# Loads, sums and row 0 of the first batch: another order in the prologue of a Fourier mixing and SwiGLU kernel

## The chip, the cores and the metric

The kernel runs on one core of a Trainium2 chip. Times are device microseconds (us) of that core. A "run" is one execution; a profile is one run with the hardware profiler on, and its span is some 2 us shorter than its time. Names: TensorE (PE; PEld its weight loads), VectorE (DVE), ScalarE (ACT), GpSimd (POOL), SyncE (SP, which here only issues DMA).

For a program on one core no die stands beside it to compare, so besides the time I always look at the **mean granted clock** of TensorE: 1.000 if it had full clock all the time, 0.997 with one stretch of half clock of 3.4 us in some 618 (half of 3.4/618 is 0.0028), 0.994 with two.

## The reference

```python
X = np.fft.fft(x, axis=1)            # x: 8 x 3008 x 256
X = np.fft.fft(X, axis=2)
x = X.real.astype(np.float32).reshape(8 * 3008, 256)
g = x @ w_gate                       # 256 x 1536
silu = g * (1.0 / (1.0 + np.exp(-g)))
return (silu * (x @ w_val)) @ w_out  # 24064 x 256
```

## The kernel before

The transform over the sequence is folded by symmetry (middle blocks XA and XC), then done with tables of cosines and sines; the transform over the 256 columns is multiplied into the weights (Wp, Wq, Wm). Then units of 512 tokens by 128 hidden columns go through TensorE, ScalarE (Silu) and VectorE, products hp and hm are multiplied with Wo, and ScalarE copies the output from PSUM into one of three buffers (ev), from which SyncE stores it. GpSimd folds the later batches and makes some of the products hm.

The prologue, where the change is (SyncE's queue is `q`; cuts are marked). `place` sends a block through TensorE in passes that reverse its order; a chunk is a slice of the weights that one load brings; `halves` makes bf16 copies of the sums:

```python
    for hi, what, eng in ((1, 2, nc.scalar), (0, 2, q), (0, 0, q), (1, 0, q), (0, 1, q), (1, 1, q)):
        eng.dma_start(**xc0(hi, what))                    # block XC of batch 0
    q.dma_start(out=XC0[NCR:64 + NCR + 1:64, 0:2, 1],     # row 0 of batch 0
                in_=rows_at(0, 0, [[2 * R * D, 2], [R * D, 2], [1, D]]))
    for hi in range(2):
        for k in range(2):                                # zero fill for the next batch's XC
            q.dma_start(out=X3c[64 * hi + NCR:64 * hi + 64, 8 * D * k:8 * D * (k + 1)],
                        in_=xf[NCR + 1:NCR + 2, :].unsqueeze(1).to_broadcast([1, 64 - NCR, 8 * D]))
    # ... (SyncE's next instructions are the next batch's XC loads)
    psA = place(XA, putA, 4, ((psG, "g"), (psV, "v")))    # TensorE reverses XA through PSUM
    warm(20)
    sums(SA, 0, XA, psA)                                  # VectorE
    # ...
    load_w(0, (1,))                                       # GpSimd's queue: weight chunks
    # ...
    weigh(0, NCE)                                         # VectorE
    psC = place(XC0, putC, 2, ((psO, "o"),))
    # ...
    load_w(1)
    sums(SC, 0, XC0, psC)
    halves(SBc, SC, 0)                                    # ScalarE
```

Two places further on matter for what follows. In the first units VectorE also makes a table of odd angles, with two operations from SBUF to SBUF:

```python
    def weigh(lo, hi):
        vts(Tab[:, 1, 1, :, lo:hi], Tab[:, 1, 1, :, lo:hi], scalar1=wC, scalar2=None, op0=Alu.mult)
    def odd_table(c, half):                               # four times
        nc.vector.tensor_copy(Tab[r, c, :, :, NCE:NCE + GH], src[:, :, ::-1] if half else src)
```

And SyncE issues in program order: one XA load of batch 1, the load br (a row of tile Qt, so after the "Qt puts", VectorE's writes to Qt), 15 more XA loads, bc, XC loads for batches 2 and 3, and among them the output stores. GpSimd's folds of XA and XC wait for those loads.

## Time and profile before

Three runs: 620.09, 620.14 and 622.67 us, median 620.14. The head of the page:

```profile
span 618.3 us, 12468 instructions
## 1 busy us (share of the span) xinstructions
PE 601.1 (97%) x4008; PEld 393.7 (64%) x4069; DVE 582.6 (94%) x1062; ACT 528.3 (85%) x1005; POOL 469.9 (76%) x430
```

TensorE is busy for 97% of the span, and from 113 to 600 us for 483.8 of 487 us; in the timeline of that stretch its idle times add up to 0.4 us (some matmul records are missing). So whatever happens, happens in the first fifth of the kernel:

| stretch | what sets the pace |
|---|---|
| to 25.57 us | the prologue; block XC waits for row 0, then goes at half clock |
| 25.57 to about 53 | VectorE, busy 23.94 of 24.43 us up to 50 |
| about 53 to 113 | TensorE nearly full, with some holes |
| from 113 | TensorE full |

One thing about the column "busy", which the rest of this document turns on: an instruction that is held up after it has started counts as busy (the same one took 0.42 us alone and 1.93 us held, below).

### The profile page before, as it was taken

What the parts mean: (1) busy time and instruction counts of PE and PEld (TensorE: products, weight loads), DVE (VectorE), ACT (ScalarE), POOL (GpSimd) and SP (SyncE); (2) the same over time, 40 slices, a digit from 0 to 9 for tenths busy, and PEclk for the clock granted to TensorE, in tenths of its full rate; (3) what the DMA queues carried; (4) which work ended last, traced back from release to release, by engine and by line L of the source; (5) the groups of instructions that cost most, each with busy time, mean ns of one, the idle gap of its engine ahead of it and who ended that gap; (6) DMA issues with size and microseconds to landing.
All of it is one profiled execution on the core that took longest, in us unless ns stands there. A gap on an engine that the chain in (4) does not pass through costs nothing.

```text
span 618.3 us, 12468 instructions
## 1 busy us (share of the span) xinstructions
PE 601.1 (97%) x4008; PEld 393.7 (64%) x4069; DVE 582.6 (94%) x1062; ACT 528.3 (85%) x1005; POOL 469.9 (76%) x430
## 2 busy tenths in 40 slices
PE   6989999999999999999999999999999999999997
PEld 4546665666666666666666666666666666666676
DVE  9699889899999999999999999999999999999992
ACT  6686666889889889998898899998998988999993
POOL 8798679899787989986988769876887344437552
PEclk9999999999999999999999999999999999999999
DMA  9843646355414323454145112135111121111112
GB/s 229 135 68 76 165 111 187 109 142 131 135 56 128 93 62 112 139 120 129 54 105 128 51 55 78 52 86 148 54 51 52 45 61 44 52 45 53 59 52 78
DMA packets 50588, 57.68 MB, mean 93 GB/s; under 512 B 7234, under 2 KB 37578, under 8 KB 50506
## 3 DMA queue, kind: packets, MB, share of 16 engines
q1 hardware_dynamic: 46915, 53.75, 31.5%
q0 software_dynamic: 3184, 2.36, 2.8%
q10 hardware_dynamic: 423, 0.77, 0.4%
q8 instruction: 32, 0.52, 0.4%
q14 instruction: 34, 0.28, 0.2%
HBM read 29.39 MB, written 24.65 MB: 87 GB/s over the span
## 4 chain that ended last, share of the span: by engine, by line
PE 84%; DVE 7%; DMA 3%; ACT 3%; issue 2%; POOL 1%; SPq 0%; DVEq 0%; ACTq 0%
PE o L1148 35%; PE g L908 23%; PE v L908 19%; DVE es L1031 2%; DMA out_dram<-ev 2%; PE g L1291 2%; PE o L1291 2%; DVE sv L1092 2%; DMA XA<-in_x_dram 1%; ACT sv L1078 1%; DVE hp L1102 1%; PE o L411 1%; POOL EOA L478 1%; PE v L1148 0%; PE o L578 0%
## 5 line engine op out<-in xcount | busy, mean ns | idle before, releaser
L1099 POOL TENSOR_TENSOR hm<-sv 128x1024 bf16<-128x1024 f32 (+2 forms) x133 | 247.5, 1861 | 119.8 <-ACT sv L1078 73.1
L1092 DVE SCALAR_TENSOR_TENSOR sv<-es,v 128x512 f32<-128x512 f32 (+2 forms) x266 | 178.5, 672 | 3.4 <-PE v L908 2.5
L1102 DVE TENSOR_TENSOR hp<-sp,v 128x512 bf16<-128x512 f32 (+2 forms) x260 | 174.6, 672 | 3.5 <-ACT sp L1075 2.2
L1148 PE MATMUL o<-Wo,hm 128*128 128x256 bf16 (+1 forms) x1128 | 166.6, 273 | 0.6
L1148 PE MATMUL o<-Wo,hp 128*128 128x256 bf16 (+1 forms) x1104 | 165.4, 273 | 0.4
L1148 PEld LDWEIGHTS <-hm 128*128 128x128 bf16 (+2 forms) x1140 | 112.0, 98 | 60.4 <-issue 0.2
L1148 PEld LDWEIGHTS <-hp 128*128 128x128 bf16 (+2 forms) x1140 | 112.1, 98 | 58.4 <-issue 1.3
L1006 ACT ACTIVATE sp<-g 128x512 f32<-128x512 f32 (+2 forms) x198 | 119.3, 603 | 30.3 <-PE g L908 19.7
L1078 ACT ACTIVATE sv<-g 128x512 f32<-128x512 f32 (+2 forms) x198 | 129.3, 655 | 5.0 <-PE g L908 3.9
L908 PE MATMUL v<-Pt,Wp 128*128 128x512 bf16 (+2 forms) x284 | 106.4, 375 | 3.8 <-DVE hm L966 1.4
L908 PE MATMUL g<-Pt,Wp 128*128 128x512 bf16 (+2 forms) x284 | 106.4, 375 | 0.7 <-DVE Qt L1308 0.3
L1031 DVE SCALAR_TENSOR_TENSOR es<-bc,w,v 128x512 f32<-128x512 bf16 (+2 forms) x140 | 102.3, 732 | 1.4 <-PE v L908 1.1
L908 PE MATMUL g<-Qt,Wq 128*128 128x512 bf16 (+2 forms) x242 | 90.3, 374 | 0.3
L980 ACT ACTIVATE v<-bc,w 128x512 f32<-128x512 bf16 (+2 forms) x126 | 87.2, 692 | 0.5 <-DVE hp L1102 0.3
L908 PE MATMUL g<-Qt,Wm 128*128 128x512 bf16 (+2 forms) x217 | 81.3, 375 | 0.6 <-ACT sp L1006 0.2
L1029 ACT COPY es<-v 128x512 f32<-128x512 f32 (+2 forms) x126 | 74.0, 587 | 2.7 <-PE v L908 2.3
L908 PEld LDWEIGHTS <-Wp 128*128 128x128 bf16 x576 | 56.2, 98 | 30.9 <-issue 5.3
L1154 ACT COPY ev<-o 128x512 f32<-128x512 f32 x89 | 53.6, 602 | 9.1 <-PE o L1148 4.7
L908 PE MATMUL v<-Qt,Wq 128*128 128x512 bf16 (+2 forms) x159 | 59.5, 375 | 0.2
L908 PEld LDWEIGHTS <-Wq 128*128 128x128 bf16 x450 | 44.0, 98 | 23.6 <-issue 2.4
L908 PE MATMUL v<-Qt,Wm 128*128 128x512 bf16 (+2 forms) x148 | 55.4, 374 | 0.6 <-DVE hp L946 0.6
L1010 DVE SCALAR_TENSOR_TENSOR sg<-bc,w,g 128x512 f32<-128x512 bf16 (+2 forms) x68 | 49.6, 729 | 0.3 <-POOL hp L1111 0.3
(187 smaller groups left out, 702.5 us busy)
## 6 DMA issues: line engine op xcount, KB each, us to landing
out_dram<-ev SPq DMA_DIRECT2D x96, 128.0 KB
XA<-in_x_dram SPq DMA_DIRECT2D x30, 256.0 KB
XA<-in_x_dram SPq DMA_DIRECT2D x112, 64.0 KB
XC<-in_x_dram SPq DMA_DIRECT2D x32, 120.0 KB
XC<-in_x_dram SPq DMA_DIRECT2D x105, 32.0 KB
bc<-br SPq DMA_DIRECT2D x21, 128.0 KB
St<-Fc SPq DMA_DIRECT2D x14, 128.5 KB
out_dram<-ev SPq DMA_DIRECT2D x12, 120.0 KB
```

Of the source, the lines that this page charges most:

```text
L908: nc.tensor.matmul(ps[:, :n], Wt[:, gv, fs], src[:, :n], start=start, stop=stop, skip_group_check=True)
L980: nc.scalar.activation(T_[kv][:, :w], bc[t][:, :w], AF.Copy, scale=w0[:, 1, f:f + 1])
L1006: nc.scalar.activation(T_[ksp][:, :w], T_[kg][:, :w], AF.Silu)
L1010: nc.vector.scalar_tensor_tensor(T_[keg][:, :w], bc[t][:, :w], w0[:, 0, f:f + 1], T_[kg][:, :w], op0=Alu.mult, op1=Alu.add)
L1029: nc.scalar.copy(T_[kes][:, :w], T_[kv][:, :w])
L1031: nc.vector.scalar_tensor_tensor(T_[kes][:, :w], bc[t][:, :w], w0[:, 1, f:f + 1], T_[kv][:, :w], op0=Alu.mult, op1=Alu.add)
L1078: nc.scalar.activation(sv()[:, f % 2, w - 1::-1, 1], T_[kgm if by_dve else kg][:, :w], AF.Silu)
L1092: nc.vector.scalar_tensor_tensor(sv()[:, f % 2, w - 1::-1, 0], T_[kes][:, :w], 2.0, T_[kv][:, :w], op0=Alu.mult, op1=Alu.subtract)
L1099: nc.gpsimd.tensor_tensor(hts_(t)[1][:, f - 1:f + 1, :w], sv()[:, :, :w, 1], sv()[:, :, :w, 0], op=Alu.mult)
L1102: nc.vector.tensor_tensor(hts_(t)[0][:, f, :wp], T_[ksp][:, :wp], T_[kv][:, :wp], op=Alu.mult)
L1148: nc.tensor.matmul(st["ps"][:n, j, :], hts[t][minus][:, f, c:c + n], Wo[:, f, :], start=(f == 0), stop=(f == nF - 1))
L1154: nc.scalar.copy(ev[:, 0:len(pair), :], st["ps"][:, 0:len(pair), :])
```

## The change

The intent: block XC of batch 0 comes earlier, because its loads are short pieces on two queues and row 0 goes by GpSimd's queue; VectorE folds it straight from PSUM; small work goes to ScalarE; the zero fill and so the next batch's loads come later. The core of the diff:

```diff
-    q.dma_start(out=XC0[NCR:64 + NCR + 1:64, 0:2, 1],
-                in_=rows_at(0, 0, [[2 * R * D, 2], [R * D, 2], [1, D]]))
-    (zero fill: four DMAs out of XC0)
+    rise_c(0, q)
+    fall_c(1, 0, nc.scalar)
+    fall_c(1, 1, nc.scalar)
+    rise_c(1, q)
+    fall_c(0, 0, q)
+    fall_c(0, 1, q)
 ...
+    nc.gpsimd.dma_start(out=XC0[NCR:64 + NCR + 1:64, 2:4, 0],
+                        in_=rows_at(0, 0, [[2 * R * D, 2], [R * D, 2], [1, D]]))
 ...
+    weigh_ce()                 (ScalarE; was weigh(0, NCE) on VectorE)
+    warm(8)
+    psC = place(XC0, putC, 2, ((psG, "g"), (psV, "v")))
 ...
-    sums(SC, 0, XC0, psC)
-    halves(SBc, SC, 0)
+    direct(0)                  (VectorE, PSUM to the bf16 halves)
+    direct(1)
+    nc.gpsimd.memset(zeros, 0.0)
+    for hi in range(2):
+        q.dma_start(out=X3c[64 * hi + NCR:64 * hi + 64, :].rearrange("p (c d) -> p c d", d=D),
+                    in_=zeros[64 * hi + NCR:64 * hi + 64].unsqueeze(1).to_broadcast([64 - NCR, 16, D]))
 ... (sums of SC, half_folded(1), load_w(1), load_w(2), heads and turns stand later;
      both Wm halves of the first weight chunk go from GpSimd to ScalarE)
```

From the first feed-forward unit on every engine's instruction order is the same in both kernels.

More of the change, by code (lines that the diff above doesn't have):

```diff
@@ L240, with fall_a, rise_c, fall_c @@
     q.dma_start(out=XA3[:, 0:4, :], in_=up_block(0, 1, P))
-    nc.scalar.activation(w0[:, 0, 0:1], zero, AF.Silu)
-    nc.scalar.dma_start(out=XA3[:, 7, :], in_=down_set(0, 3, JA, LA, NA))
-    for k in range(2):
-        nc.scalar.copy(xf[:, 4 * D * k:4 * D * (k + 1)], zero.to_broadcast([P, 4 * D]))
-    for a, eng in ((2, q), (1, nc.scalar), (0, q)):
-        eng.dma_start(out=XA3[:, 4 + a, :], in_=down_set(0, a, JA, LA, NA))
+    def fall_a(a, eng):
+        eng.dma_start(out=XA3[:, 4 + a, :], in_=down_set(0, a, JA, LA, NA))
+    def rise_c(hi, eng):
+        eng.dma_start(out=XC3[64 * hi:64 * hi + 64, 0:2, :],
+                      in_=rows_at(0, 2 * (P + 1) - 1 + 2 * hi * R, [[2 * D, 64], [R * D, 2], [1, 2 * D]]))
+    def fall_c(hi, a, eng):
+        eng.dma_start(out=XC3[64 * hi:64 * hi + NCR, 2 + a, :], in_=down_set(0, 3 - 2 * hi - a, JC, LC, NC_))
+    nc.scalar.activation(w0[:, 0, 0:1], zero, AF.Silu)
+    fall_a(3, nc.scalar)
+    nc.scalar.copy(xf[:, 4 * D:8 * D], zero.to_broadcast([P, 4 * D]))
+    fall_a(2, q)
+    fall_a(1, nc.scalar)
+    fall_a(0, q)
+    rise_c(0, q)
[4 more added lines that the diff above has]
+    fall_c(0, 1, q)
     iota = dict(channel_multiplier=0, allow_small_or_imprecise_dtypes=True)
@@ L257 @@
     nc.gpsimd.iota(pcol2, pattern=[[0, 1]], base=P, channel_multiplier=1, allow_small_or_imprecise_dtypes=True)
-    def xc0(hi, what):
-        if what == 2:
-            return dict(out=XC3[64 * hi:64 * hi + NCR, 0:2, :],
-                        in_=rows_at(0, 2 * (P + 1) - 1 + 2 * hi * R, [[2 * D, NCR], [R * D, 2], [1, 2 * D]]))
-        return dict(out=XC3[64 * hi:64 * hi + NCR, 2 + what, :], in_=down_set(0, 3 - 2 * hi - what, JC, LC, NC_))
-    for hi, what, eng in ((1, 2, nc.scalar), (0, 2, q), (0, 0, q), (1, 0, q), (0, 1, q), (1, 1, q)):
-        eng.dma_start(**xc0(hi, what))
-    q.dma_start(out=XC0[NCR:64 + NCR + 1:64, 0:2, 1],
-                in_=rows_at(0, 0, [[2 * R * D, 2], [R * D, 2], [1, D]]))
-    X3c = XC.rearrange("p a q d -> p (a q d)")
-    for hi in range(2):
-        for k in range(2):
-            q.dma_start(out=X3c[64 * hi + NCR:64 * hi + 64, 8 * D * k:8 * D * (k + 1)],
-                        in_=xf[NCR + 1:NCR + 2, :].unsqueeze(1).to_broadcast([1, 64 - NCR, 8 * D]))
     for i, c_ in enumerate((pcol, pcol2)):
@@ L282, in more_iotas @@
             nc.gpsimd.iota(putC[:, pm - NCR:pm], pattern=[[-LC, NC_], [1, LC]], base=pm - LC, **iota)
-            nc.gpsimd.memset(putC[:, pm:pm + 1], float(pm))
         pts(putC, putC, scalar1=pcol, scalar2=1.0, op0=Alu.is_equal, op1=Alu.mult)
@@ L288 @@
         ps = psO.tile([P, T], F32, name="o")
-        for j in range(10):
+        for j in range(13):
             nc.tensor.matmul(ps[:, 0:P], sel, sel, start=True, stop=True)
@@ L325 @@
     vts(sgn, half, scalar1=1.0 / 32, scalar2=1.0, op0=Alu.mult, op1=Alu.add)
+    sgo = const.tile([P, 1], F32, name="sgo")
+    vts(sgo, pc, scalar1=float(NCR), scalar2=-2.0, op0=Alu.is_equal, op1=Alu.mult)
+    vts(sgo, sgo, scalar1=1.0, scalar2=sgn, op0=Alu.add, op1=Alu.mult)
     vts(wC, pc, scalar1=float(LC - 1), scalar2=-0.5, op0=Alu.is_equal, op1=Alu.mult)
@@ L354, in opposite, with weigh_ce @@
         nc.scalar.activation(Tab[:, ch, :, :, NCE:NOO - 1], Tab[:, ch, :, :, GH + 1:NCE], AF.Copy, scale=-1.0)
+    def weigh_ce():
+        nc.scalar.activation(Tab[:, 1, 1, :, 0:NCE], Tab[:, 1, 1, :, 0:NCE], AF.Copy, scale=wC)
     def load_w(fc, only=(0, 1)):
@@ L414, in place, with sums @@
         return pss
-    def sums(S, k, X, pss):
+    def sums(S, k, X, pss, only=None):
         n = len(pss)
-        for a in range(n):
+        for a in only or range(n):
             down = X[:, 7 - a] if n == 4 else X[:, 2 + a]
@@ L447, in half_w @@
             nc.scalar.copy(dst[:, :, fs], ps)
-            pts(Wm[:, :, fs], dst[:, :, fs], scalar1=m2, scalar2=1.0, op0=Alu.mult, op1=Alu.mult)
         else:
@@ L506, in first_rows, with direct @@
         nc.scalar.copy(w0.rearrange("p g f -> p (g f)"), ps[:, 0:2 * nF])
+    def direct(k):
+        for a in range(2):
+            down = XC0[:, 2 + a, ::-1, :]
+            for hf, r_ in ((0, slice(P, 0, -1)), (1, slice(P, D))):
+                x_, y_ = psC[a][:, :, r_], down[:, :, r_]
+                if k and hf:
+                    x_, y_ = y_, x_
+                vtt(SBc[:, k, hf, a], x_, y_, op=(Alu.add, Alu.subtract)[k])
     psA = place(XA, putA, 4, ((psG, "g"), (psV, "v")))
     warm(20)
-    sums(SA, 0, XA, psA)
+    sums(SA, 0, XA, psA, (0, 1, 2))
+    sums(SA, 1, XA, psA, (0,))
+    sums(SA, 0, XA, psA, (3,))
     opposite(0)
-    for a in (0, 2):
-        fold_d(0, a)
+    fold_d(0, 0)
+    weigh_ce()
+    fold_d(0, 2)
+    opposite(1)
     load_w(0, (1,))
     d_tables()
-    sums(SA, 1, XA, psA)
+    sums(SA, 1, XA, psA, (1, 2, 3))
     start_acc(0)
     half_folded(0, 0)
-    weigh(0, NCE)
-    opposite(1)
-    psC = place(XC0, putC, 2, ((psO, "o"),))
+    warm(8)
+    psC = place(XC0, putC, 2, ((psG, "g"), (psV, "v")))
     half_folded(0, 2)
@@ L524 @@
         fold_d(1, a)
-    load_w(1)
-    sums(SC, 0, XC0, psC)
-    halves(SBc, SC, 0)
+    direct(0)
+    direct(1)
     start_acc(1)
-    for a in (0, 2):
-        half_folded(1, a)
+    X3c = XC.rearrange("p a q d -> p (a q d)")
+    zeros = Af.rearrange("p a b d -> p (a b d)")[:, 0:D]
     hd = tp.tile([P, 2, 2, 1], F32, name="hd")
     ptt(hd, SA[:, 0, 0:2, :, 0:1], SA[:, 0, 2:4, :, 0:1], op=Alu.add)
+    nc.gpsimd.memset(zeros, 0.0)
+    for hi in range(2):
+        q.dma_start(out=X3c[64 * hi + NCR:64 * hi + 64, :].rearrange("p (c d) -> p c d", d=D),
+                    in_=zeros[64 * hi + NCR:64 * hi + 64].unsqueeze(1).to_broadcast([64 - NCR, 16, D]))
     heads(nc.gpsimd, hd[:, 0], hd[:, 1], CEa)
     nc.gpsimd.tensor_copy(EOA[:, 0, :, :, P:P + 1], SA[:, 0, :, :, 0:1])
-    heads(nc.gpsimd, SC[:, 0, 0, :, 0:1], SC[:, 0, 1, :, 0:1], CEc)
-    sums(SC, 1, XC0, psC)
     nc.vector.memset(SDt[:, :, 0:1], 1.0)
-    halves(SBc, SC, 1)
-    load_w(2)
-    nc.gpsimd.iota(kfO, pattern=[[4, G]], base=1, **iota)
-    for ch in range(2):
-        turns(rrO[:, ch].bitcast(I32), kfO, ch)
     ptile, qtile = {}, {}
@@ L635 @@
     transform(0, 0, (0,), acc)
-    for q in range(2):
-        row0(0, q, acc[1][q])
+    sums(SC, 0, XC0, psC)
+    for a in (0, 2):
+        half_folded(1, a)
+    load_w(1)
+    nc.gpsimd.iota(kfO, pattern=[[4, G]], base=1, **iota)
+    heads(nc.gpsimd, SC[:, 0, 0, :, 0:1], SC[:, 0, 1, :, 0:1], CEc)
+    turns(rrO[:, 0].bitcast(I32), kfO, 0)
+    load_w(2)
+    turns(rrO[:, 1].bitcast(I32), kfO, 1)
     for k in range(2):
@@ L640 @@
     unfolded(1, SBc)
+    for q in range(2):
+        row0(0, q, acc[1][q])
+    sums(SC, 1, XC0, psC)
     transform(0, 0, (1,), acc)
@@ L643 @@
     half_w(1, 1, psO, "o")
+    for h in range(2):
+        fs = slice(h * T // 2, (h + 1) * T // 2)
+        nc.scalar.activation(Wm[:, :, fs], Wq[:, :, fs], AF.Copy, scale=m2)
     nc.gpsimd.dma_start(out=Wo, in_=moe_w_out.rearrange("(f p) d -> p f d", p=P))
@@ L653 @@
         for dst, src, sg in ((BBc[:, q, 0, 0], E[:, 0, 0:P], 1.0), (BBc[:, q, 0, 1], E[:, 1, 0:P], -1.0),
-                             (BBc[:, q, 1], O[:, :, 0:P], 1.0), (BBc[:, q, 1, 0, 0:1], S[:, 1, 0:1], -1.0),
+                             (BBc[:, q, 1], O[:, :, 0:P], None), (BBc[:, q, 1, 0, 0:1], S[:, 1, 0:1], -1.0),
                              (BBc[:, q, 1, 1, 0:1], S[:, 0, 0:1], 1.0)):
-            pts(dst, src, scalar1=sgn, scalar2=sg, op0=Alu.mult, op1=Alu.mult)
+            pts(dst, src, scalar1=sgn if sg else sgo, scalar2=sg or 1.0, op0=Alu.mult, op1=Alu.mult)
     tmp_ctx.close()
```

## The prediction

> **What bounds the kernel now.** I read the windows first, to see where a prologue ends and what follows it. Columns of a row are: stretch and length in us; busy time and count of TensorE matmuls, its weight loads, VectorE, ScalarE, GpSimd; then granted clock, DMA share, GB/s.
>
> ```profile
> 11.72:15.14 3.42, 0.98 (x5) 0.51 (x6) 3.42 (x4) 2.45 (x6) 3.40 (x4) 1.00 1.01 180
> 15.14:18.55 3.41, 3.41 (x5) 1.14 (x5) 1.23 (x2) 1.86 (x3) 2.42 (x7) 0.50 0.94 118
> 18.55:25.57 7.02, 7.02 (x53) 4.60 (x51) 4.26 (x13) 3.73 (x7) 5.16 (x10) 1.00 0.93 154
> 25.57:50.00 24.43, 22.04 (x128) 10.46 (x127) 23.94 (x44) 19.08 (x36) 22.86 (x35) 1.00 0.40 70
> 50.00:100.00 50.00, 48.34 (x314) 31.21 (x319) 43.77 (x74) 30.27 (x58) 38.25 (x41) 1.00 0.51 132
> ```
>
> From 25.57 us, where the first matmul of the feed-forward part stands, VectorE is busy 23.94 of 24.43 us; from 200 to 600 us TensorE is busy 397.2 of 400 (another answer: 198.79 and 198.43 in two stretches of 200). So what comes after the prologue has no slack worth the name: whatever the prologue saves, at VectorE and TensorE alike, should be carried to the end, and nothing more. The instruction orders of the two kernels agree that this is the only place: with line numbers and buffer numbers left out, every engine's stream is the same after the first feed-forward unit. The whole change is worth what it takes from 25.57.
>
> Then the timeline of the prologue, TensorE alone (start, length, instruction; the bracket is idle time before it):
>
> ```profile
> 9.85 1.28 PE L437 MATMUL o<-sel 128*128 128x128 bf16 x20
> 12.28 0.49 PE L466 MATMUL v<-Tab,EOb 128*128 128x377 bf16 x2 [1.15 <-ACT EOb L479]
> 12.61 0.48 PE L466 MATMUL g<-Tab,EOb 128*128 128x377 bf16 x2
> 14.98 3.60 PE L411 MATMUL o<-XC,putC 128*128 128x512 f32 x4 [1.88 <-POOL EOA L478]
> 18.37 0.58 PE L466 MATMUL v<-Tab,EOb 128*128 128x377 bf16 x2
> 22.53 0.61 PE L445 MATMUL o<-W,CD 128*128 128x256 bf16 x4
> 25.57 0.37 PE L908 MATMUL g<-Pt,Wp 128*128 128x480 bf16 x1
> ```
>
> The prologue loses time at L411, which puts the middle block XC of batch 0 in reverse order. It starts at 14.98 after a hole of 1.88, and takes 3.60 for four passes. The releaser named, GpSimd EOA, is not what it needs: its waits in the program are two rise loads of XC, the row-0 load, an old PE count and putC, which GpSimd had finished at 7.69. The trace's DMA semaphore records put the rises at 11.20 and 11.69 and row 0 at 14.81. So the last wait is row 0, because SyncE issues it last:
>
> ```profile
> 3.19 5.91 SPq L266 DMA_DIRECT2D XC<-in_x_dram  x5
> 10.26 0.60 SPq L267 DMA_DIRECT2D XC<-in_x_dram  x1
> 10.90 2.79 SPq L272 DMA_DIRECT2D XC<-XC  x4
> 13.74 12.17 SPq L140 DMA_DIRECT2D XC<-in_x_dram  x15
> ```
>
> The 3.60 is 0.9 a pass; the same shape took 0.43 (3.5 us for eight passes, from 6.34) before. After L411 the chain is TensorE without a hole to 25.57.
>
> **What the Trainium skill says.** "TensorE: Matmul & The Clock Gate", section "What's actually happening": the array runs at half clock after a window of some 3.4 us without enough work, and at full clock after a busy one. The trace agrees: 0.98 busy of 3.42 from 11.72, then 0.50 granted for exactly the next 3.41, the stretch of L411. "DMA: Bandwidth & Descriptors", section "Why a DMA increments its semaphore by 16 and not by 1": a transfer on these queues uses only as many of the 16 engines as divide its outer dimensions, the lowest-numbered ones. The trace agrees: of the second fc-0 weight load eleven engines reported by 17.4 and five between 18.1 and 19.6; of the last fc-2 load twelve by 25.7, four between 29.7 and 31.75. Those four also carry the four-partition loads L272 and L140. "VectorE: DVE Perf Modes", section "Why PSUM operands drop a tier": float32 from PSUM has no fast mode. The trace agrees: 128x512 sums step by 0.60, so I price a 128x256 one at 0.33 (estimate: half of 0.53, the element part, plus 0.07).
>
> **Part by part.** Durations are those of before; waits are read from the built program.
>
> 1. *Row 0 on GpSimd's queue, no one-element memsets.* Row 0 is issued at 5.44 (end of the turns) and should land far ahead of need. GpSimd pays 0.74 for the issue, less some 0.4 for the two memsets: its chain is later by 0.35, so the first weight load is issued from 9.85 to 10.8 and the first EOA starts at 10.8 instead of 10.46.
> 2. *VectorE up to the sums.* Two small ones for sgo add 0.24: first sum at 8.78. A 1-sum is put in fourth, so sum 3 ends at 11.78 and the eighth at 13.58; that is 0.60x8. EOA 0: 10.8 to 11.87; EOA 2: to 12.94; weight issue to 13.68; EOA of the differences to 14.77 and 15.84.
> 3. *TensorE to L411.* EOb 0 at 11.95 to 12.57; its four matmuls 12.63 to 13.3; eight dummies to 13.85. The place of XC follows at once, since its loads (two rises, no lane wait for the first) are in by about 12, in full clock: 2x0.86, to 15.6, against 18.6 before. Of the 3.0 won here, 1.1 is the earlier start and 1.9 the clock.
> 4. *ScalarE.* Weighing goes from VectorE (2.34) to ScalarE (about 0.9), the four halves copies (2.1) go. EOb 2 ends 13.9, opposite to 14.65, the four table steps to 16.0, EOb of the differences 16.6 and 17.1.
> 5. *VectorE folds from PSUM.* Eight at 0.33: two from 14.85, two from 15.65, four to 17.6. TensorE: EOb 2 15.6 to 16.2, unfolded 0 to 17.5 (2x0.64), both differences to 18.8, two half_w to 19.7, unfolded 1 to 21.0, row0 (0.75) to 21.75, two half_w (0.9) to 22.65.
> 6. *What must be ready beside it.* Pt puts 17.65 to 18.9, sums of SC to 20.1, CEc at 20.5 (needed 21.0); Wp copy 20.75; second sums 21.95; Qt puts 22.0 to 23.3; second Wp copy 23.95. ScalarE: second Wq copy 23.3, then both Wm copies (moved from GpSimd, 2x0.55) to 24.4; the first Silu's matmul ends at 24.3.
>
> So the feed-forward part starts at 22.65 instead of 25.57, and the first hp on VectorE at 25.5 (after the two angle steps of 1.60 from 23.95) instead of 28.47:
>
> ```profile
> 26.35 0.68 DVE L450 CAST Wp<-o 128x512 bf16<-128x512 f32 x1
> 26.95 1.60 DVE L338 SCALAR_TENSOR_TENSOR XA<-XA,mM 128x376 f32<-128x376 f32 x2
> 28.47 1.21 DVE L946 TENSOR_TENSOR hp<-sg,v 128x480 bf16<-128x480 f32 x2
> ```
>
> Both say 2.9 us. In before VectorE is then full to 50 us, each hp directly behind its own earlier work, so the shift holds if the matmuls between are not stopped by something new. More dummy matmuls at the start (12 at about 0.06) end before the rises of XA land at 6.21 and cost nothing.
>
> 7. *Chunk loads of the weights, the term I am least sure of.* GpSimd gets to the fc-1 loads after EOA, hd, a memset and the heads: issue ends 17.75 and 18.45 (before 16.14 and 16.86); the fc-2 loads come after CEc and two turns: 22.4 and 23.15 (before 20.41 and 21.13). The semaphore records of before show them landed 6.5, 8.8, 7.4 and 10.6 us after that. TensorE first reads them at 26.41, 30.38, 32.70 and 35.53; 2.9 earlier is 23.5, 27.5, 29.8, 32.6. With the old latencies they land at 24.2, 27.2, 29.8, 33.8: the first 0.7 and the last 1.2 late. Against that, the four slow engines have no zero fill and no next-batch load until about 16.5 (the fill waits for GpSimd's memset), where before they carried them from 10.9, and the new fill is in 1 KB pieces. But those loads then also run on to about 30 rather than 26, beside the fc-2 chunks. I take half of the mean of the two, some 0.4 us, as lost.
>
> Sum: 620.14 - 2.9 + 0.4 = 617.6 us, a gain of 0.4%.
>
> **The rivals.** *The late chunk takes the place of row 0.* TensorE takes its instructions in order, so a wait of 1.2 for the last fc-2 chunk holds up the matmuls behind it, and VectorE, being full, can't make it good; if the slow engines are as loaded as before plus the fc-2 overlap, 2 us go: about 619.3. For it: four engines late by up to 6 us in before. Against it: 3.8 to 4.9 us of slack there now, and an emptier start. *The clock falls anyway.* The windows of before have edges at 11.72, 15.14 and 18.55; if a window with EOb's hole in it is judged idle, the 3 us behind it double, less what waits anyway: 1.5 to 2 lost, about 619.3 too. Against it: from 11.72 to 15.14 I count 0.8 of matmuls, 0.5 of dummies and 1.3 of the place, 2.6 of 3.4. *The new bound is ScalarE*, which takes weighing and both Wm copies: the first Silu at 24.45, behind Wm, leads hp's turn at 25.5 by only 0.5 us after its own 0.57; if a copy takes 0.7 instead of 0.55 there is still 0.2 left, so I give it nothing. *More is won*, if the sums and the fold of XC lie closer than I put them or GpSimd's issue of row 0 takes less: about 616.8. *Nothing changes*, if VectorE's work in the first units is fed late by something the orders don't show: 620.
>
> **Range and chances.** The main sum is a chain of traced durations with an error of perhaps 0.5; the weight chunks can take from 0 to 2; medians of three runs differ by some 0.1, though one run of before was 2.5 longer. So 616.6 to 619.2. A change of 2% is 12.4 us, and the entire prologue has 25.6: faster by that is next to impossible, and slower would need a stall four times the savings.
>
> **What would show it.** Step 1: row 0's semaphore full well before 13 us, and no hole ahead of XC's place other than that for EOb. Step 3: the four passes of the place in about 1.7 to 1.8 us, granted clock 1.00 there, first pass near 13.9. Step 5: eight VectorE folds of some 0.33. Steps 5 and 6: the first feed-forward matmul near 22.7 and the first hp near 25.5. Step 7: the wait of TensorE ahead of each of the four chunk reads; over 0.5 at any makes my 0.4 too small. It would be wrong if the first feed-forward matmul moved by 2.9 and the end by less than 1.5, or if the first units of the two kernels differed by something other than these waits.

## The result, and the profile after

The changed kernel took 614.46, 614.67, 614.92 and 615.51 us, median 614.79; before, in the same rounds, 620.09 to 624.43, median 621.4. The ratio is 0.9888, 95% interval 0.9846 to 0.993. Ratios here are the mean time of one kernel's fast runs over that of the other's of the same rounds, so not quite the ratio of the medians. It is a gain of 1.1%, some 7 us by the means of these rounds (621.8 and 614.9); I had said 617.6 and at best 616.6. The head of the page after, then the windows of its prologue (columns as in the prediction):

```profile
span 612.7 us, 12572 instructions
## 1 busy us (share of the span) xinstructions
PE 603.9 (99%) x4089; PEld 394.9 (64%) x4089; DVE 582.1 (95%) x1071; ACT 526.5 (86%) x1003; POOL 468.9 (77%) x428
```

```profile
11.72:15.14 3.42, 2.48 (x16) 1.51 (x17) 1.99 (x4) 3.12 (x6) 3.40 (x5) 1.00 1.03 171
15.14:18.55 3.41, 3.41 (x21) 1.90 (x20) 3.36 (x13) 2.35 (x6) 3.39 (x9) 1.00 0.54 78
18.55:22.63 4.08, 4.08 (x35) 2.94 (x33) 4.03 (x11) 1.06 (x2) 2.36 (x6) 1.00 0.88 131
```

And TensorE's timeline, the two pairs of passes for XC and the first feed-forward matmul:

```profile
13.76 1.08 PE L419 MATMUL g<-XC,putC 128*128 128x512 f32 x2
14.67 1.02 PE L419 MATMUL v<-XC,putC 128*128 128x512 f32 x2
...
22.63 0.37 PE L936 MATMUL g<-Pt,Wp 128*128 128x480 bf16 x1
```

XC is placed from 13.76 at full clock, and the feed-forward part starts at 22.63. I had predicted 13.85 to 13.9 and 22.65. So the prologue is as foreseen, and the rest of the gain comes after it. I compared the two traces instruction by instruction on VectorE (the orders are the same there). How far the changed kernel leads:

| at (us of before) | lead, us | what lies between |
|---|---|---|
| 25 | 2.94 | the prologue |
| 31.8 | 3.66 | |
| 42.5 | 4.97 | the weighing of the odd table |
| 49.2 | 4.90 | the Qt puts |
| 56.3 | 3.14 | the copies of the odd table |
| 59.6 to 92.7 | 3.66 | |
| 115.7 to the end | 5.32 | two output copies, at 94 and 111 |

Three steps, then: 2.0 won from 25 to 49 us, 1.2 lost from there to 60, 1.7 won between 93 and 116. The last has two parts: at TensorE, 0.7 at the copy at 94 and 1.0 at that at 111.

**The step at 42.** All engines in the timeline of before, cut to two lines:

```profile
40.00 2.35 POOL L157 TENSOR_TENSOR SDf<-XC 64x1020 f32<-64x1020 f32 x1
...
40.63 1.93 DVE L351 TENSOR_SCALAR Tab<-Tab,wC 128x752 bf16<-128x752 bf16 x1
```

and the same of after:

```profile
37.05 0.42 DVE L354 TENSOR_SCALAR Tab<-Tab,wC 128x752 bf16<-128x752 bf16 x1
...
42.00 2.35 POOL L157 TENSOR_TENSOR SDf<-XC 64x1020 f32<-64x1020 f32 x1 [4.80 <-DMA XC<-in_x_dram]
...
49.88 3.34 DVE L1428 COPY Tab<-Tab 64x752 bf16<-64x752 bf16 x2
...
50.65 2.35 POOL L157 TENSOR_TENSOR SDf<-XC 64x1020 f32<-64x1020 f32 x1
```

The same weighing takes 0.42 us alone and 1.93 beside GpSimd's fold, and ends 0.2 us after it. In the changed kernel the fold waits 4.80 us for the next batch's loads, which are late now, so VectorE slips past. The Trainium skill, "SBUF — State Buffer", section "SBUF: two separate sides", says that VectorE and GpSimd share one pair of ports as an exclusive lock: a GpSimd operation excludes an operation of VectorE that runs in a 2-port fast mode (or that has two inputs in SBUF, if GpSimd's reads SBUF too) for a whole instruction, and whichever starts second waits. The trace agrees: 0.42 against 1.93. VectorE's products, which read PSUM, take 0.64 beside the fold as elsewhere. The step back, to 3.14, is the same thing in the other direction: two copies that took 1.07 in before take 3.34 beside the changed kernel's second fold.

**The step after 93.** Here TensorE depends on an output copy of ScalarE, the seventh of the kernel (the expectations below call it the third). Lines of before from the timeline, SyncE, GpSimd, ScalarE, TensorE:

```profile
49.71 0.59 SPq L1419 DMA_DIRECT2D br<-Qt  x1
...
91.09 1.21 SPq L1160 DMA_DIRECT2D out_dram<-ev  x3
...
92.78 2.35 POOL L157 TENSOR_TENSOR SDf<-XC 128x1020 f32<-128x1020 f32 x1 [3.69 <-DMA XC<-in_x_dram]
94.14 0.59 ACT L1154 COPY ev<-o 128x512 f32<-128x512 f32 x1 [2.03 <-DMA out_dram<-ev]
94.78 0.33 PE L1291 MATMUL o<-Tab,CEa 128*128 128x189 bf16 x2 [0.69 <-ACT ev L1154]
```

and of after:

```profile
44.80 0.61 SPq L1447 DMA_DIRECT2D br<-Qt  x1
...
85.99 1.21 SPq L1188 DMA_DIRECT2D out_dram<-ev  x3
...
87.25 2.35 POOL L157 TENSOR_TENSOR SDf<-XC 128x1020 f32<-128x1020 f32 x1 [2.68 <-DMA XC<-in_x_dram]
...
89.81 0.59 ACT L1182 COPY ev<-o 128x512 f32<-128x512 f32 x1 [1.36 <-PE o L1176]
```

In before ScalarE's output copy at 94.14 has waited 2.03 for a store to free its buffer, and TensorE 0.69 for the copy. The store was issued at 91.09, as SyncE has all the XC loads ahead of it, and these go back without a break to br at 49.71. From br to the store it is 41.4 us in before and 41.2 in after: a **second path**, which starts when VectorE has put Qt. In after it starts 4.9 us earlier, and the copy no longer waits for it.

The 1.0 at 111 is something else. Lines of before, ScalarE and TensorE:

```profile
111.00 0.59 ACT L1154 COPY ev<-o 128x512 f32<-128x512 f32 x1 [1.16 <-PE g L908]
112.21 0.36 PE L908 MATMUL v<-Pt,Wp 128*128 128x480 bf16 x1 [0.85 <-ACT v L980]
```

In after the same copy, at 105.60, has no wait ahead of it. By the semaphore records a store from its buffer, issued between 103.45 and 104.50, had all its parts in only at 110.90: one of its 16 parts came some 2.4 us behind the other 15. The two later traces of before (b_look1, b_look2) don't have this hole of TensorE, nor does any edited kernel's but a_early's (0.62, at 115.07). So I take it for an accident of the one trace that I compared with, and not an effect of the change. Against those two the changed kernel wins 1.9 each at the copy at 94 to 97 and nothing at 111.

### The profile page after: what moved, and what is told of

The parts are those of the page before. It is cut to its first block, busy times and chain, and to the rows that moved or that the text cites. A ratio compares the mean times of both kernels' runs of the same rounds, so it can differ in the third digit from the quotient of the medians.

```text
span 612.7 us, 12572 instructions
## 1 busy us (share of the span) xinstructions
PE 603.9 (99%) x4089; PEld 394.9 (64%) x4089; DVE 582.1 (95%) x1071; ACT 526.5 (86%) x1003; POOL 468.9 (77%) x428
## 4 chain that ended last, share of the span: by engine, by line
PE 91%; DVE 3%; ACT 2%; POOL 1%; issue 1%; DMA 1%; ACTq 0%; DVEq 0%; POOLq 0%; SPq 0%
PE o L1176 38%; PE g L936 26%; PE v L936 19%; PE g L1319 2%; PE o L1319 2%; PE v L1176 1%; DMA bc<-br 1%; DVE es L1059 1%; PE g L593 1%; DVE sv L1120 1%; PE o L593 0%; DVE hp L1130 0%; ACT sg L971 0%; DMA br<-Qt 0%; PE o L453 0%
## 5 line engine op out<-in xcount | busy, mean ns | idle before, releaser
L936 PE MATMUL v<-Pt,Wp 128*128 128x512 bf16 (+2 forms) x288 | 107.9, 375 | 0.6 <-DVE hm L994 0.6
L936 PE MATMUL g<-Pt,Wp 128*128 128x512 bf16 (+2 forms) x288 | 107.9, 375 | 0.3 <-ACT sv L1106 0.2
L936 PE MATMUL g<-Qt,Wq 128*128 128x512 bf16 (+2 forms) x288 | 107.6, 375 | 0.0
```

The costliest lines, as they stand in the source:

```text
L936: nc.tensor.matmul(ps[:, :n], Wt[:, gv, fs], src[:, :n], start=start, stop=stop, skip_group_check=True)
```

## The experiments

Two theories at the start. **T**: the extra gain comes from VectorE's fast operations that meet GpSimd's folds or don't. **R**: it is made between 92 and 113 us alone. In the course a third came up, **S**: two paths run from the Qt puts, VectorE with TensorE, and SyncE with GpSimd; the later one sets the time at 93 to 106 us.

All results were right. "Mean" is that of the six runs of a kernel; the kernel before had means of 621.2, 621.8, 620.6 and 620.9 in the four batches.

### First batch: the collisions

**a_again**, the changed kernel without an edit.

> The changed kernel again, unedited, as the mark for the others of this call. Theory T (the collision): the prologue gives 2.9 us and about 2.4 more come because VectorE's weighing of the odd table at 37 us is no longer held by GpSimd's fold (0.42 instead of 1.93 us), so the gain is 5 to 6 us: ratio 0.990 to 0.992. Rival N (the runs of before were merely slow): the gain comes out near 3 us, ratio 0.995.

Measured 614.71 median (613.42 to 615.51), ratio 0.9898, interval 0.9873 to 0.9923. The gain stands. In this run's trace the two copies took 2.30, not 3.34, and it ended 1.1 us earlier than the first trace.

**b_late**, the kernel before with the late loads only:

```diff
-    (zero fill: four DMAs out of XC0, early)
+    nc.gpsimd.memset(zeros, 0.0)          (behind hd, as in the changed kernel)
+    (zero fill from zeros)
```

> The kernel before, with only the zero fill and the next-batch loads made late as in the changed kernel (the fill waits for GpSimd's memset). Theory T: GpSimd's first fold step waits for these loads until after 42 us, so VectorE's weighing near 40.6 takes 0.42 to 0.6 us instead of 1.93 and VectorE leads by about 1.4 us behind it; end 1.0 to 2.0 us earlier than before, 0.997 to 0.998. Rival R (the extra gain is made between 92 and 113 us by the output stores alone): VectorE may lead at 43 us, but the end moves by less than 0.4 us. Against both, the later loads may collide with the weight chunks and cost up to 0.5.

Measured 617.08 median, mean 617.25, ratio 0.9939 (0.9914 to 0.9965). Two lines of its timeline:

```profile
40.52 0.42 DVE L345 TENSOR_SCALAR Tab<-Tab,wC 128x752 bf16<-128x752 bf16 x1
...
43.04 2.34 POOL L157 TENSOR_TENSOR SDf<-XC 64x1020 f32<-64x1020 f32 x1 [3.26 <-DMA XC<-in_x_dram]
```

VectorE's lead over before jumps from 0.12 to 1.49 there, as T says, and is 1.73 to 91 us. It falls to 1.2 with a hole of 1.21 at the output copy near 94, and is 2.2 from 113 on only by before's accident at 111. R's 0.4 falls. The prologue of this kernel is that of before, half clock and all. The mean gains 4.0, more than the trace (2.6 in span); before has more runs with two half-clock stretches, six of eleven against one of six. It is also more than T's 1.0 to 2.0. At full clock it is 2.5: three runs with a mean of 616.9, against 619.5 of the eight such runs of before in all batches.

**b_weigh_act**, the weighing of the odd table on ScalarE:

```diff
-        S.add("DVE", 0.45, lambda: weigh(NOO, NTAB), ...)
+        S.add("DVE", 0.45, lambda: nc.scalar.activation(Tab[:, 1, 1, :, NOO:NTAB],
+              Tab[:, 1, 1, :, NOO:NTAB], AF.Copy, scale=wC), ...)
```

> The kernel before, with only the weighing of the odd table moved from VectorE to ScalarE, nothing else. Theory T: 1.93 us go from VectorE, so it leads by 1.4 to 1.9 us at 43 us; the end is 1.0 to 1.9 us earlier, ratio 0.997 to 0.998. Rival R: end within 0.4 us of before. ScalarE pays about 1 us at a time at which it then idles 1.15, so no loss there.

Measured 620.28 median, ratio 0.9984 (0.9956 to 1.0013): the mean gains 1.2, and the interval holds zero and T's 1.0 to 1.9 alike, so the times decide nothing. The trace says where T's gain went. The lead is 0.79 before the place of the weighing (this run had full clock in the prologue) and 2.18 right behind it, so the 1.4 were won; then hm and hp wait 0.38 and 0.69 for ScalarE, which now does the weighing, and the next copy takes 1.82 instead of 1.45; the lead is 0.93. It ends at 1.91, but 1.0 of this is before's accident at 111 again. To move work is not to remove it.

**a_collide**, a collision put in by hand: GpSimd gets a useless addition in its idle gap, and VectorE's weighing comes one product later so that it falls into it.

```diff
+                if (fc, gv) == (2, 1):    (behind GpSimd's last Wm)
+                    ptt(SDf[64:P].rearrange("p a d -> p (a d)")[:, 0:1020],
+                        Wp[64:P, 0, 0:1020], Wp[64:P, 1, 0:1020], op=Alu.add)
```

> The changed kernel with a useless GpSimd addition (64x1020, two operands in SBUF, about 2.3 us) put into GpSimd's idle gap from 37.2 us, and VectorE's weighing one product later so that it falls into it; GpSimd's fold itself stays at 42.0. The result stays right. Theory T: the weighing takes 1.8 to 2.3 us instead of 0.42; VectorE loses 1.4 to 1.9 us of its lead and the end is 1.0 to 1.9 us later than that of the changed kernel. Rival R: the weighing may stretch, but the end stays within 0.4 us.

```profile
37.21 2.12 POOL L1385 TENSOR_TENSOR SDf<-Wp 64x1020 f32<-64x1020 bf16 x1
...
37.97 1.57 DVE L354 TENSOR_SCALAR Tab<-Tab,wC 128x752 bf16<-128x752 bf16 x1
```

The weighing ends 0.21 behind the addition, as it did behind the fold. Median 617.6, mean 618.1 against 614.66 of the changed kernel: 3.4 lost, or 2.2 if only runs of clock 0.999 and more are taken (616.89, four runs). Again more than the collision itself, 1.15. Its trace has the lost time made good by 58 us (lead 0.21) and back again at 93, with a hole of TensorE of 1.17 at the same output copy: br had been issued at 46.08 instead of 44.80. That is what led to theory S.

### Second batch: the parts of the change alone

**a_no_warm**, the changed kernel without the eight dummy matmuls (`-    warm(8)`).

> The changed kernel without the eight dummy matmuls ahead of XC's place (some 0.5 us of TensorE work). Theory C (the dummies keep the clock): the stretch of 3.4 us that ends near 15 us then has too little work in some or all runs, the granted clock falls to 0.5 for the next 3.4 us, and such runs show a mean clock of 0.997 instead of 1.000 and end 0.8 to 1.9 us later. Rival (the earlier place alone keeps the clock): clock 0.999 to 1.000 in all runs and the time within 0.5 us of the changed kernel.

Median 615.05, mean 615.43, against 614.66 in the first batch; five of six runs at 0.999 or 1.000, one at 0.996 with 618.3. In the trace TensorE is busy for 2.14 of 3.40 us from 11.7 to 15.1 and keeps full clock. So the rival holds nearly always: the earlier place is enough. Where the one slow-clock run lost its stretch isn't known; it has no trace.

**b_row0_gp**, the kernel before with row 0 on GpSimd's queue:

```diff
-    q.dma_start(out=XC0[NCR:64 + NCR + 1:64, 0:2, 1], in_=rows_at(...))
+    nc.gpsimd.dma_start(out=XC0[NCR:64 + NCR + 1:64, 0:2, 1], in_=rows_at(...))   (behind turns)
```

> The kernel before with row 0 alone moved to GpSimd's queue, nothing else. As predicted in step 3: the place of XC starts 1.5 to 1.9 us earlier (near 13.3 instead of 14.98) and at full clock, and the first feed-forward matmul comes 1.5 to 2.7 us earlier than 25.57; the runs have a clock of 0.999 to 1.000 throughout, and the mean falls by 2 to 3.5 us, since the mean of before contains runs with half-clock stretches. Rival: behind the place VectorE's sums and ScalarE's halves of XC are the path, as a run of a sibling kernel at full clock showed (place at 15.19 in 1.96 us, first feed-forward matmul only at 24.81), and less than 1 us comes of it.

Median 620.6, ratio 0.9977 (0.9949 to 1.0004). The place starts at 13.27, full clock, and the first feed-forward matmul comes at 23.35: this one line makes 2.2 of the prologue's 2.9. VectorE then leads by 2.28 from 50 to 77 us. And then:

```profile
95.08 0.59 ACT L1154 COPY ev<-o 128x512 f32<-128x512 f32 x1 [4.51 <-DMA out_dram<-ev]
95.71 0.33 PE L1291 MATMUL o<-Tab,CEa 128*128 128x189 bf16 x2 [3.18 <-ACT ev L1154]
```

```profile
92.70:96.10 3.40, 0.39 (x4) 0.32 (x4) 0.96 (x2) 1.02 (x3) 2.53 (x3) 1.00 0.50 133
96.10:99.50 3.40, 3.40 (x14) 1.75 (x13) 2.20 (x8) 1.57 (x4) 3.40 (x3) 0.52 0.50 111
```

The store comes late, TensorE stands for 3.18 us, has only 0.39 us of work in a stretch of 3.4, and gets half clock for the next one (second line, 0.52). (In the stretch that ends just where the clock falls, 92.84 to 96.25, it is 0.54.) The lead of 2.28 becomes a lag of 2.5 from 98 us on, 1.5 at the end by before's accident at 111. This is my prediction's sentence refuted in one trace: a saving of the prologue was *not* carried to the end. br is issued at 47.45, 2.26 earlier than in before, and the store at 91.95, 0.86 later: from one to the other it is 44.5 us here and 41.4 there. The first output store, some 17 us behind br, already comes 3.0 later; the loads before it took longer to issue in this run (12 XA loads 6.63 us against 5.78). The rest of the expectation failed too: the mean fell by 1.4, not by 2 to 3.5, and five of six runs have clock 0.996 to 0.997.

**a_early**, the changed kernel with zero fill and next-batch loads early again:

```diff
+    nc.vector.memset(Af..., 0.0)          (at the start)
     fall_c(0, 1, q)
+    (zero fill from Af, then the next batch's loads)
-    (zero fill behind hd)
```

> The changed kernel with the zero fill and the next-batch loads early again (zeros from a memset of VectorE at the start, fill and loads right behind the falls in SyncE's order). Theory T (what counts is only which of VectorE's fast copies meets GpSimd's work): GpSimd's first fold then starts near 37.3, just after VectorE's weighing at 37.05, which stays at 0.42; its second fold starts near 45.9 and ends before the two copies at 49.9, which then take about 1.1 to 1.5 instead of 2.3 to 3.3; end 0.5 to 1.5 us earlier than the changed kernel. Rival (late loads are good in themselves, they keep DMA engines free for the weight chunks): TensorE waits over 0.5 us for chunks of fc-1 or fc-2, and the end is 1 us or more later.

Median 621.7, mean 621.87, ratio 1.0002 (0.997 to 1.0034): everything gone. Theory T had expected a gain and is wrong about this part; the rival was right, even too mild. From TensorE's timeline:

```profile
22.62 0.58 PE L459 MATMUL o<-W,CD 128*128 128x256 bf16 x2 [3.36 <-DMA W<-in_moe_w_val_dram]
...
27.64 0.37 PE L936 MATMUL g<-Pt,Wp 128*128 128x480 bf16 x1
```

TensorE waits 3.36 us for the second weight chunk, then goes at half clock, and the feed-forward part starts at 27.64, 5.0 later than in the changed kernel. VectorE's weighing collided as well (1.66 us at 42.72). So loads as early as here delay the weights. That every early load does isn't shown: these are issued from 11.50, ahead of before's (13.74), while b_row0_gp, with its loads from 13.06, began its feed-forward part at 23.35.

**a_copies_act**, the changed kernel with the four copies of the odd table on ScalarE (`nc.vector.tensor_copy` becomes `nc.scalar.copy`).

> The changed kernel with the four copies of the odd table (64x752 each) on ScalarE instead of VectorE. Theory T: VectorE loses 3.9 to 5 us of copies, most of it time held by GpSimd, and leads by 2 to 3 us at 54 us; ScalarE pays four times about 0.9. If VectorE's lead is carried, the end is 1 to 2 us earlier than the changed kernel. Rival (ScalarE paces there once it has this work, as when it took the weighing): VectorE waits for ScalarE for over 1 us between 45 and 55 us, and the end moves by less than 0.5 us.

Median 617.98, mean 617.53, so 2.9 later in mean: neither T's 1 to 2 us earlier nor the rival's 0.5. TensorE led the changed kernel by 0.6 to 1.4 from 54 to 86 us, and was 3.7 behind from 95: a hole of 2.74 at the same output copy and half clock from 93 to 96. A faster VectorE made the kernel slower in four of six runs (618.88 at clock 0.996 to 0.997; 614.83 in the two at 1.000).

### Third batch: take away the wait for the store

A fourth output buffer, in the end of a scratch tile that nothing uses after 42 us; no engine's order changes, and GpSimd's fold waits for the XC loads alone, as before.

```diff
-            st["ev"] = ev = evp.tile([P, 2, D], F32, name="ev")
+            st["ev"] = ev = SDf[:, 4:6, :] if n_ev[0] % 4 == 3 else evp.tile([P, 2, D], F32, name="ev")
+            n_ev[0] += 1
```

**b_ev4** (before with it):

> The kernel before with a fourth buffer for the output copies (the free end of the scratch tile SDf), every engine's order unchanged. Theory S (two chains run from the Qt puts near 45 to 49 us: TensorE and VectorE to the third output copy near 94, and SyncE's loads and stores to the store that frees the buffer of that copy; the later one decides): the copy near 94 no longer waits 2.03 for a store, TensorE's hole of 0.69 there goes, and where SyncE is later than in that profile (3.18 of hole in a sibling kernel, with a half-clock stretch behind it) more goes. Mean 1 to 2 us below before, no more runs of clock 0.993 to 0.995. Rival N (the low-clock runs of before come from chance elsewhere): mean within 0.5 us, clocks as before.

**a_ev4** (the changed kernel with it):

> The changed kernel with the fourth output buffer. Its third output copy waits for TensorE, not for a store (89.81, 1.36 of idle put down to TensorE), so theory S expects no change: within 0.5 us of 614.7. Rival (stores wait further on in both kernels): 1 us or more earlier.

**a_copies_ev4** (with the copies on ScalarE too):

> The changed kernel with the copies of the odd table on ScalarE and the fourth output buffer. Without the buffer VectorE and TensorE led by 1.0 to 1.4 us to 86 us and lost it, and more, at a hole of 2.74 us and the half-clock stretch behind it. Theory S: with the buffer the hole goes, the lead stays, and this is the fastest of all: 1.0 to 2.0 us below the changed kernel, clock 0.999 to 1.000. Rival (the loads of XC for GpSimd's fold, not the store, hold TensorE there): hole and half-clock stay, 617 to 618.

**b_row0_ev4** (before, row 0 on GpSimd's queue, and the buffer):

> The kernel before with row 0 on GpSimd's queue and the fourth output buffer. Without the buffer a lead of 2.28 us stood until 77 us and was lost at a hole of 3.18 and a half-clock stretch at 95 to 99. Theory S: the lead now stays: 1.5 to 3 us below the fourth-buffer kernel of before, 617 to 618, clock 0.999 to 1.000. Rival: within 0.7 us of the same kernel without the buffer (620.6).

| kernel | median | mean | ratio (interval) |
|---|---|---|---|
| b_ev4 | 619.96 | 620.60 | 0.9998 (0.9966 to 1.0031) |
| a_ev4 | 615.13 | 616.00 | 0.9924 (0.989 to 0.9959) |
| a_copies_ev4 | 615.49 | 615.40 | 0.9915 (0.9887 to 0.9942) |
| b_row0_ev4 | 618.99 | 618.38 | 0.9957 (0.9925 to 0.9989) |

The hole at the output copy near 94 went in all of them, as S says: in b_ev4 the copy stands at 93.52, after an idle 1.36 put down to TensorE, and TensorE leads before by 0.62. The gain did not stay. What held TensorE next, in b_row0_ev4:

```profile
97.85 1.89 POOL L1099 TENSOR_TENSOR hm<-sv 128x1024 bf16<-128x1024 f32 x1
...
100.52 0.38 PE L908 MATMUL v<-Pt,Wp 128*128 128x512 bf16 x1 [2.59 <-DVE sv L1092]
```

GpSimd's product hm stands in its order behind the XC fold and two more fold steps, the fold waits for the XC loads, VectorE and ScalarE wait for the product to free a buffer sv, and TensorE for them: 2.59 of hole (1.35 in b_ev4), and half clock from 101. So the path holds TensorE in two ways, by the store and by the fold; I had called the second a rival and taken away only the first. b_ev4's prediction of 1 to 2 us failed, and the low clocks of before remained. a_ev4 stayed within its 0.5 us in the median, not in the mean (two runs at 0.997). a_copies_ev4 gained over a_copies_act in mean, 617.5 to 615.4, but in another batch, and was not 1 to 2 us below the changed kernel, as expected. b_row0_ev4 is 2.2 below b_ev4 in mean, as S had it, but above its 617 to 618, and three of six runs have 0.997.

### Fourth batch: start the second path earlier

Fifteen XA loads of batch 1 issue ahead of br instead of behind it; SyncE idled there. Only SyncE's order changes.

```diff
-            loads[0:0] = ((("A", 1), k, fn) for k, fn in enumerate(load_a(1, nc.sync)))
+            fns = load_a(1, nc.sync)
+            first = [lambda: [g() for g in fns[:NA]]] + [lambda: None] * (NA - 1)
+            loads[0:0] = ((("A", 1), k, fn) for k, fn in enumerate(first + fns[NA:]))
```

**b_xaord** (before with it):

> The kernel before with the fifteen XA loads of batch 1 ahead of the first br load in SyncE's order (where they stood behind it, SyncE idled from 38 to 49.7 us), all other orders unchanged. Theory S: SyncE's next loads start near 52 instead of 58.6, GpSimd's first XA fold near 62 to 64 instead of 68.4, its XC fold at 87 to 90 instead of 92.8; no hole of TensorE between 90 and 112 (0.69, 0.15 and 0.85 before), no half-clock stretch there, so no more runs of clock 0.993 to 0.995; mean 1.5 to 3 us below before, 0.995 to 0.9975. Rival (the path does not matter, what is lost after 90 us comes from elsewhere): mean within 0.5 us.

**b_row0_xaord** (and row 0 on GpSimd's queue):

> The same with row 0 on GpSimd's queue besides. Theory S: the lead of about 2 us that this part alone made at 25 us now stays to the end: 1.5 to 2.5 us below the kernel with the loads' order alone, 616 to 617, clock 0.999 to 1.000. Rival: within 1 us of it, as without the order (618.8 to 622).

**a_xaord** (the changed kernel with it):

> The changed kernel with the same order of loads. Here GpSimd's folds are late anyway (XC's second one frees XC at 53.3, SyncE is there at 53.8), so theory S expects little: the XA fold 0 to 1 us earlier, no change of the end, within 0.5 us of 614.7. If the early XA loads delay the XC loads that land near 42, up to 1 us is lost.

**a_xaord_copies** (and the copies of the odd table on ScalarE):

> The changed kernel with the order of loads and the copies of the odd table on ScalarE. Theory S: the lead of 1.0 to 1.4 us that these copies make to 86 us is lost only where SyncE's path is later than TensorE's; the path gains 0.5 to 1 us by the order, so about half of the lead stays: 613.5 to 614.5, and some runs may still fall to a clock of 0.997 and 617. Rival (the copies do not matter): 614.7.

| kernel | median | range | mean | ratio (interval) |
|---|---|---|---|---|
| b_xaord | 618.8 | 618.47 to 619.8 | 619.04 | 0.9973 (0.9946 to 1.0) |
| b_row0_xaord | 617.01 | 615.35 to 617.11 | 616.57 | 0.9936 (0.991 to 0.9961) |
| a_xaord | 614.56 | 613.74 to 615.48 | 614.57 | 0.9903 (0.9878 to 0.9929) |
| a_xaord_copies | 613.42 | 613.19 to 613.92 | 613.50 | 0.9886 (0.9862 to 0.991) |

S holds in the traces and nearly to the numbers, though b_xaord's own interval touches 1.0. In b_xaord the store is issued at 84.97 and the XC fold starts at 87.58 (91.09 and 92.78 in before), and of TensorE's holes from 90 to 112 us only two of 0.25 and 0.15 are left. Row 0, worth 1.4 us in mean without this order and not surely more than nothing, is worth 2.5 with it. From b_row0_xaord:

```profile
85.05 2.35 POOL L157 TENSOR_TENSOR SDf<-XC 128x1020 f32<-128x1020 f32 x1
...
92.61 0.58 ACT L1154 COPY ev<-o 128x512 f32<-128x512 f32 x1 [1.36 <-PE o L1148]
```

Both paths meet with time to spare, and all six runs have a clock of 0.999 or 1.000. The changed kernel gains nothing by the order, as expected, until its copies go to ScalarE: then the 1.3 us that TensorE leads by at 67 us are still there at 124, and the six runs lie within 0.7 us. At 613.42 this is the fastest of all; it was timed beside before and a_xaord (means 613.50 and 614.57), not beside the unedited changed kernel, whose ten runs elsewhere were 613.42 to 615.51.

One miss: b_xaord was to have no more runs at 0.993 to 0.995, and had two at 0.994. Its own trace has that clock, and both stretches lie in the prologue, from 14.3 to 21.1.

### Two looks at the kernel before

> The kernel before, unedited, for its trace alone. If its mean clock is 0.993 to 0.995, theory S expects at least one of the 3.4 us stretches of half clock between 92 and 106 us, behind a hole of TensorE of over 1 us at the third output copy; the rival is that both lie between 12 and 22 us. If it is 0.997 there is one stretch, and it tells only which of the two places it has.

> The same once more, since about half of the runs of this kernel have the low clock. Same expectation.

The first took 619.18 (clock 0.997), the second 621.88 (0.994). Windows of the second:

```profile
10.70:14.10 3.40, 1.03 (x8) 0.35 (x5) 2.96 (x6) 2.06 (x5) 3.38 (x4) 1.00 1.14 214
14.10:17.50 3.40, 2.09 (x3) 1.09 (x4) 0.01 (x1) 2.24 (x5) 3.31 (x6) 0.50 0.85 99
17.50:20.90 3.40, 3.40 (x9) 1.19 (x9) 2.39 (x4) 0.98 (x2) 1.30 (x6) 0.50 0.99 164
```

Both stretches lie in the prologue: the first begins at 14.1, the place of XC only at 15.41, so this stretch is itself not full (2.09 of 3.40), and the next is at half clock as well. The first feed-forward matmul comes at 27.02. In the first look it came at 24.44, because the place started at 13.85; in the trace I predicted from, 25.57. In these three traces of one kernel the half-clock stretch begins at 14.1, 14.0 and 15.1: its edges fall differently in each run. S's late stretch did not show here, only in edited kernels; both looks have a hole of 1.9 at the output copy near 94 to 97, where the first trace had 0.69, and neither has its hole at 112.

## Why the prediction was wrong

Its steps, in its own order.

**Steps 1 to 6, the prologue: right.** The first feed-forward matmul was predicted at 22.65 and came at 22.63, the first hp at 25.5 and came at 25.36. The folds took 0.33 to 0.41 each. (I hadn't derived the split of 0.60 into 0.53 and 0.07 that my 0.33 rests on; the folds do step by 0.33, from 16.40 to 17.40.) The split of the 3.0 us was wrong in detail: I gave 1.9 to the clock, but in the trace of b_weigh_act the place goes at full clock from 15.19 and the feed-forward part still starts only at 24.81, so full clock alone was worth 0.8 there.

**Step 7, the weight chunks: the size met by luck.** One wait of 0.41 in the trace of the changed kernel, at 29.71, which is the third of the four reads; I had put 0.7 at the first and 1.2 at the last, and neither waited. Nor was it lost to the end: VectorE's lead is 3.66 at 31.8 of before and 3.65 at 35. In three relatives the wait is 0.80 to 0.93, in two of these with a second of 0.45 and 0.48. That the late parts of a weight load come from the engines that carry the four-partition loads was inferred: the records show four of sixteen parts late (29.73 to 31.75, the others by 25.70), not which engines. The late loads, which I listed as relief against this term, are worth more than I gave them where the alternative is as early as in a_early.

**The step that failed: "whatever the prologue saves, at VectorE and TensorE alike, should be carried to the end, and nothing more".** It was wrong in both halves.

*"Nothing more".* I read VectorE's 23.94 busy of 24.43 us as work that can only shift. 1.5 us of it was the weighing, held by GpSimd (1.93 in place of 0.42), and the change made GpSimd's fold 2.0 us later and VectorE's weighing 3.6 us earlier, so they no longer met; b_late and a_collide show it from both sides. That a changed start of transfers changes what meets what was not among my rivals. A sign stood in the trace that I read: the prologue's own weighing of nearly this shape (128x754) took 2.34 and ended 0.23 behind a GpSimd operation beside it. Of the 2.0 us won from 25 to 49 us this explains 1.3; most of the other 0.7 lies at an angle step that took 1.12 us in before and 0.57 in after, beside the same short operation of GpSimd. Before, then after:

```profile
30.75 0.73 POOL L180 TENSOR_TENSOR BBa<-EOA 128x256 bf16<-128x256 f32 x1
30.76 1.12 DVE L342 TENSOR_SCALAR SDf<-XA 128x752 int32<-128x752 int32 x1
```

```profile
27.65 0.57 DVE L345 TENSOR_SCALAR SDf<-XA 128x752 int32<-128x752 int32 x1
27.78 1.04 POOL L180 TENSOR_TENSOR BBa<-EOA 128x256 bf16<-128x256 f32 x1
```

Whichever started second is the longer one, so I take it for the same thing, but no run tests it.

*"Carried to the end".* Between 93 and 106 us TensorE depends on the second path. A lead survives there only if the second path ends earlier too: it has to be won before the Qt puts, which start both paths, and the path must not take longer. The changed kernel won 4.9 before them and its path took 41.2 us, so both moved. The 1.2 that it then lost to held copies were lost to the end: in the trace of a_again, where these copies took 2.30 and not 3.34, TensorE is 1.0 ahead of the first trace from 54 us on and still at the end. In a_copies_act a lead of 1.4 was won behind the Qt puts, and the second path took it away, with a clock penalty on top. In b_row0_gp 2.28 were won ahead of them, and went all the same, because the path took 44.5 us. b_row0_xaord and a_xaord_copies show such leads kept once SyncE's loads start earlier.

**The size, and the base.** From trace to trace it is 5.6 us of span: 2.9 as predicted, and by the failed step 2.0 won to 49 us, 1.2 lost to held copies and 0.7 won at the copy at 94; then 1.0 by what I take for an accident at 111 and 0.3 behind the last matmul (the parts are rounded). The 2.9 is one draw as well: the feed-forward part starts at 25.57 in this trace of before, at 24.44 and 27.02 in the two looks. From mean to mean it is more, 621.1 (44 timed runs of before in the four batches) to 614.75. By mean clock, the 44 runs are:

| mean clock | runs | mean, us |
|---|---|---|
| 0.999 to 1.000 | 8 | 619.5 |
| 0.996 to 0.997 | 18 | 620.2 |
| up to 0.995 | 18 | 622.8 |

All ten timed runs of the changed kernel lie at 0.999 or 1.000. At full clock the difference is 619.5 less 614.75, 4.7; the rest of the 6.4, 1.7, goes with the half-clock stretches that 36 of 44 runs of before have and none of these ten. I had counted one stretch, from one trace. "Medians of three runs differ by some 0.1" was too narrow as well: runs of before went from 618.2 to 624.9.

**What stays open.** Why SyncE needs 40.5 us from br to the store in one run and 44.5 in another, with the same instructions; it waits for earlier transfers at nearly every issue, but I have no run that changes only that. Nor why one part of a store came 2.4 us late in the first trace of before. And the share of before's low-clock runs that have their second stretch at 93 to 106 us: none of its own three traces has it there.

## What to carry to other kernels

A busy engine isn't the same as a bound: compare each operation's time with that of the same shape elsewhere in the trace, since time held by another engine counts as busy, and a change that shifts one engine can set it free or catch it. Before carrying a saving to the end, look for the next place where another engine's chain, above all an in-order queue that mixes loads and stores, meets the one that was sped up, and ask from which event that chain starts; only what is won ahead of that event can move both, and even that is lost where the second chain takes longer. And where the clock depends on how full a free-running stretch of 3.4 us is, one trace is one draw: count the clocks of all runs first.

## What the Trainium skill lacked or had wrong

- "TensorE: Matmul & The Clock Gate", section "What's actually happening", gives the length of the window and that it is free-running (the traces agree), but not how full it must be. Here stretches of 3.4 us that end where the clock falls had 0.54 (b_row0_gp), 1.05 (b_look2) and 1.39 us of matmuls (b_ev4, 12.47 to 15.88); two of 2.09 and 2.43 us of matmuls at half clock (b_look2, b_xaord) did not bring full clock back. a_no_warm kept full clock with 2.14 from 11.7 to 15.1, but where its stretches begin isn't known.
- "SBUF — State Buffer", section "SBUF: two separate sides", has the lock, and the runs agree (0.42 alone; 1.93, 1.66 and 1.57 behind a GpSimd operation of 2.1 to 2.35). It does not say that the profile counts the held time as busy time of the waiting engine, which is what misled me.
- No page that I cite says what a store costs that stands in one in-order queue behind loads: here 40.5 to 44.5 us from br to the store, and up to 4.51 us of wait for it at the output copy.
